# A linear-attention and gated-FFN kernel: the first segment with tokens on partitions, and every engine's list made anew

## The chip, the cores and the metric

The kernel runs on one core of a Trainium2 chip, as one program. The metric is the device time of an execution in microseconds. The engines are TensorE (PE, with its weight loads PEld), VectorE (DVE), ScalarE (ACT), GpSimd (POOL) and SyncE (SP), which issues all DMAs here.

## The reference

Four batches, eight heads, 768 tokens, head size 48. A complex decay is clamped in magnitude, a state of 48x48 per head runs over the tokens, and its output goes through a gated FFN (d_model 384, d_ff 1024) with a three-tap convolution over the tokens.

```python
mag = np.sqrt(a_re * a_re + a_im * a_im)
scale = np.minimum(mag, 0.999) / (mag + 1e-06)
a_re_n, a_im_n = (a_re * scale, a_im * scale)
for t in range(S):
    new_re = ar * S_re - ai * S_im
    new_im = ar * S_im + ai * S_re
    kv = np.einsum('bhd,bhe->bhde', k[:, :, t], v[:, :, t])
    S_re, S_im = (new_re + kv, new_im)
    y[:, :, t] = np.einsum('bhd,bhde->bhe', q[:, :, t], S_re)
...
h = np.maximum(x @ w_in, 0.0)
for k in range(K):
    conv_out += conv_w[k][None, None, :] * hp[:, k:k + S, :]
gate = 1.0 / (1.0 + np.exp(-conv_out))
return (h * gate @ w_out).astype(np.float32)
```

## The kernel before

The recurrence is computed in chunks of 128 tokens. The decays become running sums: of the logarithm of the magnitude, and of the angle. A k or q is multiplied by the exponential of the log sum and by cosine and sine of the angle sum; then a chunk is ordinary causal attention (scores, mask, values) and a state that is carried from chunk to chunk.

Two chunks, 256 tokens, make a segment; there are twelve, three per batch. A segment goes through `a_pre` (load a, squares), `a_log` (logarithms, their running sum, table of logarithms and exponentials), `a_trig` (arctangent), `c_pre` (running sum of the angle, reduced to turns), `c_exp` (exponentials of plus and minus the log sum, times q and k) and `c_post` (cosine, sine, the products `qkc_t`). In nearly all segments channels lie on the partitions (16 channels of each of 8 heads, three groups `g`), and a running sum is a scan along the free dimension on DVE. The first two segments, those in `CUM`, have tokens on the partitions when a is loaded and make their sums as matmuls with a triangle of ones (`sums`, L460), which puts channels on the partitions in the result.

The attention needs q and k with head channels on the partitions (`stk`, 96 rows by head by token). `c_post` gets there through DRAM: it writes `qkc_t` to `qkd` (L596) and reads it back rearranged into `stk` (L598), once for k and once for q. `c_chunk` also transposes k on PE (L612) to `kn`, tokens on partitions, for the state matmuls (L619). `attention` (L656) does scores (L652), mask (L667), values and state (L676), and writes the FFN's input as a high and a low half: `x[0]` by a copy on ACT (L702), `x[1]` by a subtraction on DVE (L703).

The FFN works in ten units of 256 or 384 tokens (`UNITS`); each has four steps, a front (`moe_front`: x times w_in L758, Relu, convolution) and a back (`moe_back`: tanh, gate, times w_out L793). Unit 0 can begin when the token behind its last one is there, that is after chunk 2, the first of segment 1. The weights are loaded and split into high and low halves in the first 75 us (`load_weights`): of 16 splits the first 8 (`WHI`, all of w_in) make their high half on DVE (L387), the others on ACT (L389).

The order of the instructions on each engine is written out by hand: `ORDER` lists them by number for PE, DVE, ACT, POOL and SP, and `in_order` chains them. The first two segments are done eagerly (`FASTP`), and segments run ahead of the units that need them. The ACT's tables are loaded where a listed function needs another one.

Buffers that count here: one for a (`AB`), one for qk (`QB`), two for `qkc_t` (`QC`), three for `stk` (`TB`), two banks for `ps` (`PSA`), which transposes, scores and outputs share.

Of the kernel before, what the change touches and what calls it, by code (L numbers as in the profile page):

```python
# [14 lines left out]
I32 = mybir.dt.int32  # L15
# [63 lines left out]
CUM = [0, 1]  # L79
GROUPS = [1]*len(SEGS)  # L80
# [22 lines left out]
WHI = 8  # L103
# [59 lines left out]
    "DVE": [105, 24, 106, 111, 57, 112, 107, 63, 58, 59, 28, 113, 69, 29, 70, 109, 71, 60, 64, 65, 117, 46, 66, 72,  # L163
# [92 lines left out]
def in_order(tc):  # L256
# [4 lines left out]
    for eng, line in ORDER.items():  # L261
        last, run, sets = None, None, {}
        for k in line:
            if found[k][1]:
                both = [t for t in run[1] if t in found[k][1]] if run else []
                run = (run[0], both) if both else (k, list(found[k][1]))
                sets[run[0]] = run[1][0]
# [809 lines left out]
```

## Time and profile before

| | |
|---|---|
| median of 3 runs | 385.73 us (384.69 to 386.15) |
| profiled execution | 385.09 us |
| its span, first to last instruction | 383.3 us |
| mean granted TensorE clock | 0.971 |
| moved by DMA | 81.12 MB |
| ACT table loads | 42 (41 of them placed by `in_order`, L272) |

Busy time says what share of the span an engine had an instruction in it; matmuls are pipelined, and a busy PE is not a PE at its peak. A row of the timeline gives start, duration, engine, line and tiles, and in brackets how long the engine had been idle and what ended that. "Landing" is the time from the issue of a DMA to its completion.

### The profile page before, as it was taken

Reading aid. Unit: us, or ns where it says so; the run is one execution under the profiler, and the core shown is the slowest. Engines: PE = TensorE matmul, PEld = TensorE weight load, DVE = VectorE, ACT = ScalarE, POOL = GpSimd, SP = SyncE. Lnnn points to the kernel's source line nnn. Section 1 sums busy time; section 2 is a strip of 40 time slices with the busy share of each in tenths; the row PEclk is TensorE's granted clock in tenths of the full one; section 3 lists DMA queues with packets and bytes.
Section 4 is the critical chain, followed back from the end, with each engine's and each line's share of the span. In section 5 each row is a group of like instructions: output and inputs, shape, how many; then the busy total and the mean of one; then the engine's idle time right before and its main releaser. Section 6 shows DMA issues by size and latency. Waiting matters only on the chain.

```text
span 383.3 us, 12048 instructions
## 1 busy us (share of the span) xinstructions
PE 345.3 (90%) x5220; PEld 323.5 (84%) x5220; DVE 337.3 (88%) x552; ACT 333.1 (87%) x566; POOL 6.9 (2%) x42
## 2 busy tenths in 40 slices
PE   2577277899999999999999999999999999999993
PEld 1566275789999999999998998999999899999993
DVE  3999999989999989999999989898999988567680
ACT  5999999989999999999999998999999965346561
POOL 5000000000000000000000000000000000000000
PEclk9989758999999999999999999999999999999999
DMA  7999989995894957975959566974849828101011
GB/s 285 346 365 345 246 290 254 313 225 198 316 265 165 271 132 292 280 210 235 250 170 289 120 234 264 218 236 167 213 146 301 284 109 213 53 3 65 1 44 50
DMA packets 33423, 81.12 MB, mean 212 GB/s; under 512 B 2128, under 2 KB 23632, under 8 KB 31824
## 3 DMA queue, kind: packets, MB, share of 16 engines
q1 hardware_dynamic: 33360, 80.25, 68.4%
q8 instruction: 43, 0.70, 0.8%
q14 instruction: 20, 0.16, 0.1%
HBM read 56.65 MB, written 23.59 MB: 209 GB/s over the span
## 4 chain that ended last, share of the span: by engine, by line
PE 83%; ACT 7%; DVE 6%; issue 1%; DMA 1%; DVEq 0%
PE h_ps L758 27%; PE o L793 27%; PE ps L676 10%; PE ps L652 9%; PE s_ps L619 4%; PE ps L612 3%; PE o L471 2%; ACT w_t L420 2%; ACT L272 1%; ACT x_t L420 1%; DMA a_t<-in_at 1%; DVE qkc_t L592 1%; ACT w_t L484 1%; DVE p_t L667 1%; DVE x_t L497 0%
## 5 line engine op out<-in xcount | busy, mean ns | idle before, releaser
L793 PE MATMUL o<-wo,hg 128*128 128x384 f32 x576 | 122.3, 342 | 0.5 <-issue 0.4
L758 PE MATMUL h_ps<-x,wi 128*128 128x258 f32 (+1 forms) x720 | 122.4, 308 | 0.0
L758 PEld LDWEIGHTS h_ps<-x,wi 128*128 128x128 f32 x720 | 109.2, 189 | 1.1 <-ACT h_t L762 0.3
L793 PEld LDWEIGHTS o<-wo,hg 128*128 128x128 f32 x576 | 98.6, 188 | 3.1 <-issue 1.1
L272 ACT ACT_TABLE_LOAD x41 | 52.6, 1283 | 0.7
L652 PE MATMUL ps<-stk 96*64 96x128 f32 (+1 forms) x768 | 39.8, 257 | 9.9 <-DMA stk<-qkd 8.2
L652 PEld LDWEIGHTS ps<-stk 96*64 96x64 f32 x768 | 36.0, 142 | 14.8 <-ACT kn L613 10.8
L420 ACT ACTIVATE g_t<-g_t,cw 128x256 f32<-128x256 f32 (+1 forms) x80 | 42.5, 550 | 5.1 <-DVE g_t L765 4.9
L763 DVE SCALAR_TENSOR_TENSOR g_t<-h_t,cw 128x256 f32<-128x256 f32 (+1 forms) x80 | 41.6, 532 | 5.1 <-ACT h_t L762 4.9
L762 ACT ACTIVATE h_t<-h_ps 128x258 f32<-128x258 f32 (+1 forms) x80 | 33.5, 426 | 13.4 <-PE h_ps L758 13.1
L765 DVE SCALAR_TENSOR_TENSOR g_t<-h_t,cw,g_t 128x256 f32<-128x256 f32 (+1 forms) x80 | 41.8, 533 | 1.1
L592 DVE TENSOR_TENSOR qkc_t<-w_t,zz_t 128x1536 f32<-128x1536 f32 x24 | 41.7, 1751 | 0.3
L777 DVE SCALAR_TENSOR_TENSOR g_t<-g_t,h_t 128x512 f32<-128x512 f32 (+1 forms) x40 | 31.6, 791 | 5.7 <-ACT g_t L420 5.6
L786 DVE TENSOR_TENSOR hg<-g_t,hg 128x512 fp32r<-128x512 f32 (+1 forms) x40 | 31.6, 791 | 2.5 <-ACT hg L783 2.4
L783 ACT ACTIVATE hg<-g_t 128x512 fp32r<-128x512 f32 (+1 forms) x40 | 28.5, 716 | 5.9 <-DVE g_t L777 5.5
L667 DVE TENSOR_TENSOR p_t<-ps,mask 128x384 f32<-128x384 f32 x48 | 26.1, 552 | 7.4 <-PE ps L652 6.3
L676 PE MATMUL ps<-p_t,v_t 128*32 128x64 f32 x1344 | 25.7, 223 | 2.6 <-issue 1.7
L676 PEld LDWEIGHTS ps<-p_t,v_t 128*32 128x32 f32 x1344 | 23.0, 112 | 3.7 <-issue 2.2
L676 PE MATMUL ps<-stk,s_sb 96*32 96x128 f32 x640 | 22.1, 275 | 0.6 <-issue 0.4
L612 PE MATMUL ps<-ident,qkc_t 128*128 128x128 f32 x120 | 20.2, 289 | 1.4 <-DMA stk<-qkd 1.1
L484 ACT ACTIVATE w_t<-a_t 128x1536 f32<-128x1536 f32 x12 | 17.9, 1489 | 3.9 <-DMA a_t<-in_at 3.9
L577 DVE TENSOR_TENSOR w_t<-w_t,qk_t 128x1536 f32<-128x1536 f32 x12 | 21.0, 1752 | 0.0
(100 smaller groups left out, 450.8 us busy)
## 6 DMA issues: line engine op xcount, KB each, us to landing
qkd<-qkc_t SPq DMA_DIRECT2D x24, 768.0 KB, 4.2
stk<-qkd SPq DMA_DIRECT2D x24, 768.0 KB, 7.6
v_t<-in_v SPq DMA_DIRECT2D x12, 1024.0 KB, 8.7
qk_t<-in_qk SPq DMA_DIRECT2D x12, 768.0 KB, 6.0
a_t<-in_a SPq DMA_DIRECT2D x10, 768.0 KB, 5.1
out<-os_t SPq DMA_DIRECT2D x24, 192.0 KB, 4.5
hg<-in_w_out SPq DMA_DIRECT2D x8, 384.0 KB, 5.4
h_t<-in_w_in SPq DMA_DIRECT2D x8, 384.0 KB, 4.9
```

What stands on the lines that cost most here:

```text
L272: row = [nc.scalar.preload_act_table_set(sets[k]).ins] + row
L420: nc.scalar.activation(out, in_, func=func, **kw)
L592: nc.vector.tensor_tensor(out=qkc, in0=e[:, q:q + 1].broadcast_to([128, 2, NG * w]), in1=zz, op=ALU.mult)
L612: nc.tensor.transpose(tr[:, g - lo], kv[:, g // NG, g % NG], ident)
L652: nc.tensor.matmul(o, lhsT=kt[:, 2 * i + u, part * HC + r:part * HC + r + TM], rhs=qt[:, 2 * i + u, part * HC:C], start=first, stop=part = ...
L676: nc.tensor.matmul(yp[r0:r0 + 32, q // 4, cols], lhsT=left, rhs=right, start=r0 not in started, stop=stop, tile_position=(0, r0), skip_gro ...
L758: nc.tensor.matmul(hp, lhsT=wi[iw][:, f, kt], rhs=x[ix][:, kt], start=(k == 0), stop=(k == 8))
L762: nc.scalar.activation(h, hp, func=AF.Relu)
L763: nc.vector.scalar_tensor_tensor(out=g, in0=h[:, 0:n], scalar=cw[:, f, 0:1], in1=h[:, 1:n + 1], op0=ALU.mult, op1=ALU.add)
L765: nc.vector.scalar_tensor_tensor(out=g, in0=h[:, 2:n + 2], scalar=cw[:, f, 2:3], in1=g, op0=ALU.mult, op1=ALU.add)
L777: nc.vector.scalar_tensor_tensor(out=g, in0=g, scalar=1.0, in1=h[:, :, 1:n + 1], op0=ALU.add, op1=ALU.mult)
L793: nc.tensor.matmul(ops[t][:min(C, n - t * C)], lhsT=hg[:, k, t * C:min((t + 1) * C, n)], rhs=w[:, fw], start=(f == 0 and i == 0), stop=(f ...
```

## The change

Segment 0 alone (`TOK = [0]`) keeps tokens on the partitions up to the end. Its a and its q and k (`qk0`) come laid out by token from the host. Its running sums have the triangle as the stationary operand (`token_sums`, two output tiles, one per chunk), and the totals that later chunks need come from small matmuls (`totals`). The carry at the start of a batch, a constant, is now the bias of the exponentials instead of a matmul; segment 1 keeps its carry matmuls. q and k by heads come from PE transposes, four heads at a time, evacuated by ACT (k) and DVE (q); there is no write to DRAM and no read back for this segment, and the untransposed k serves the state matmuls as it is. The two chunks of the segment are produced and attended to one after the other. The a tile of segment 0 is loaded and squared in two halves. The first table load is put in front of ACT's first instruction. All high halves of weights are made on ACT (`WHI = 0`). Units, segments and buffers are as before; `ORDER` is a new list for every engine.

```diff
+TOK = [0]
-WHI = 8
+WHI = 0
...
+        if sets:
+            sets[line[0]] = sets.pop(next(iter(sets)))
...
+    base = {1: filled("base", SIGN * L0), -1: filled("nbase", -SIGN * L0)}
...
+    def token_sums(x, tiles):
+        xv = x.rearrange("t (k c) -> t k c", k=2)
+        for k in range(2):
+            for i in range(k + 1):
+                nc.tensor.matmul(tiles[k], lhsT=tri[0][:, (k - i) * C:(k - i + 1) * C], rhs=xv[:, i], start=i == 0,
+                                 stop=i == k)
+        return tiles
+    def totals(x, ps):
+        xv = x.rearrange("t (k n g) -> t k n g", k=2, g=NG)
+        ends = ps.shape[2]
+        for g in range(NG):
+            for k in range(2):
+                c0 = k if ends == 2 else 0
+                nc.tensor.matmul(ps[:, g, c0:], lhsT=xv[:, k, :, g], rhs=tri[0][:, C - 1::C][:, c0 + 2 - ends:],
+                                 start=k == 0, stop=k == 1, skip_group_check=True)
...
-            nc.sync.dma_start(at_, at0[CUM.index(p)])
+            for i in range(2) if p == 0 else (slice(0, 2),):
+                nc.sync.dma_start(at_[:, i], at0[CUM.index(p)][:, i])
...
-        nc.scalar.activation(w, at_, func=AF.Square)
+        for i in range(2) if p == 0 else (slice(0, 2),):
+            nc.scalar.activation(w[:, i], at_[:, i], func=AF.Square)
...
+        if p in TOK:
+            nc.vector.tensor_tensor(out=w[:, 1], in0=w[:, 1], in1=w[:, 0], op=ALU.subtract)
+            st["l", p] = token_sums(w[:, 1], [psO.tile([128, 512], F32, name=f"o{k}")[:, 0:CH] for k in range(2)])
...
+            totals(w[:, 1], ends)
+            nc.scalar.activation(cl[:, b, :, j + 1:j + 1 + m], ends, func=AF.Identity, bias=base[1])
...
+            tiles = token_sums(x[:, 0], [psH.tile([128, 512], F32, name="h_ps")[:, 0:CH] for k in range(2)])
...
+    def c_token(p, k, e, zz):
+        b, j, m = segs[p]
+        if k == 0:
+            st["stk"] = [at.tile([128, H, PR], F32, name="stk", bufs=TB)[0:96] for q in range(2)]
+        stk, found = st["stk"], {}
+        for q in (1, 0):
+            x = sc.tile([128, 2, NG * PR], F32, name="qkc_t", bufs=QC).rearrange("p c t -> p (c t)")[:, 0:2 * CH]
...
+            for i in range(2):
...
+                tr = psA.tile([128, 4, 128], F32, name="ps")
+                for h in range(4):
+                    nc.tensor.transpose(tr[0:96, h], found[q][:, 4 * i + h], ident)
+                d = stk[q][:, 4 * i:4 * i + 4, k * C:(k + 1) * C]
+                if q:
+                    nc.scalar.copy(out=d, in_=tr[0:96])
+                else:
+                    nc.vector.tensor_copy(d, tr[0:96])
...
+        c_chunk(b * NC + j + k, None, [s[:, :, k * C:(k + 1) * C] for s in stk], st["v"], found[1])
```

In the new SP list both halves of a come first, then the weights; the load of `qk0` stands behind the first five loads of w_in and four of w_out, and the load of v for segment 0 behind the last of w_in. In the new ACT list the Arctan of segment 0 comes before the last logarithm and the log sums.

## Rows read from the trace of the kernel before

**Rows 1.** The page, busy us (share of the span) and instructions.
```profile
PE 345.3 (90%) x5220; PEld 323.5 (84%) x5220; DVE 337.3 (88%) x552; ACT 333.1 (87%) x566; POOL 6.9 (2%) x42
```

**Rows 2.** Stretches: length, busy us by engine, PE clock, DMA share, GB/s.
```profile
33.00:50.00 17.00, 6.21 (x85) 5.24 (x85) 16.39 (x29) 16.79 (x25) 0.00 (x0) 0.81 0.96 268
50.00:67.00 17.00, 13.87 (x310) 11.40 (x306) 16.53 (x29) 16.11 (x24) 0.00 (x0) 0.70 1.06 286
75.00:300.00 225.00, 222.64 (x3512) 210.85 (x3513) 213.70 (x319) 220.69 (x370) 1.23 (x12) 1.00 0.76 228
```

**Rows 3.** The chain of waits: start us, us, what.
```profile
0.80 4.57 DMA a_t<-in_at
5.38 1.48 ACT w_t L484
...
115.02 0.81 PE ps L612 x6
...
368.49 8.47 PE o L793 x48
```

**Rows 4.** Timeline, ACT and PE, up to the first front.
```profile
0.80 1.28 ACT L484 ACT_TABLE_LOAD   x1 [0.80 <-PEq L1067]
...
6.88 1.28 ACT L272 ACT_TABLE_LOAD   x1
...
13.53 2.90 PE L471 MATMUL o<-tri,w_t 128*128 128x256 f32 x8 [8.08 <-DVE w_t L502]
...
16.49 1.48 ACT L484 ACTIVATE w_t<-a_t 128x1536 f32<-128x1536 f32 x1 [0.59 <-DMA a_t<-in_at]
...
19.68 1.49 ACT L420 ACTIVATE w_t<-w_t 128x1536 f32<-128x1536 f32 x1 [0.40 <-DVE gm L485]
...
20.94 2.13 PE L471 MATMUL o<-tri,x_t 128*128 128x256 f32 x12
...
32.25 0.17 ACT L395 ACTIVATE cl<-o 128x2 f32<-128x2 f32 x1 [0.30 <-PE o L471]
...
61.87 0.49 ACT L702 ACTIVATE x<-ps 128x384 fp32r<-128x384 f32 x1 [0.76 <-PE ps L676]
...
72.33 0.49 ACT L702 ACTIVATE x<-ps 128x384 fp32r<-128x384 f32 x1
...
74.91 2.40 PE L758 MATMUL h_ps<-x,wi 128*128 128x258 f32 x18
```

**Rows 5.** Timeline of SP, and the stk tile from 45 to 75 us.
```profile
50.99 0.32 SPq L596 DMA_DIRECT2D qkd<-qkc_t  x1
...
53.40 5.49 SPq L598 DMA_DIRECT2D stk<-qkd  x2
...
DMA to landing us min/median/max: 8.3/9.1/10.8
```

**Rows 6.** Groups by line and shape: busy us, mean ns.
```profile
L592 DVE TENSOR_TENSOR qkc_t<-w_t,zz_t 128x1536 f32<-128x1536 f32 x24 | 41.7, 1751 | 0.3
...
L613 ACT COPY kn<-ps 128x512 f32<-128x512 f32 x20 | 12.1, 603 | 0.1
...
L613 ACT COPY kn<-ps 128x256 f32<-128x256 f32 x20 | 8.0, 400 | 0.0
...
L389 ACT ACTIVATE wo<-hg 128x384 fp32r<-128x384 f32 x8 | 4.1, 517 | 0.0
...
L387 DVE TENSOR_SCALAR wi<-g_t 128x384 fp32r<-128x384 f32 x8 | 2.8, 356 | 0.0
```

**Rows 7.** The page, DMA issues of the whole run: KB, median us to landing.
```profile
qkd<-qkc_t SPq DMA_DIRECT2D x24, 768.0 KB, 4.2
stk<-qkd SPq DMA_DIRECT2D x24, 768.0 KB, 7.6
```

More of the change, by code (lines that the diff above doesn't have):

```diff
@@ L108 @@
 ORDER = {
[54 rows of a table removed]
-    "DVE": [105, 24, 106, 111, 57, 112, 107, 63, 58, 59, 28, 113, 69, 29, 70, 109, 71, 60, 64, 65, 117, 46, 66, 72,
[26 rows of a table removed]
-    "ACT": [23, 26, 27, 25, 30, 108, 152, 114, 199, 202, 38, 41, 37, 43, 203, 40, 206, 42, 156, 154, 201, 159, 161,
[26 rows of a table removed]
-    "POOL": [186, 2, 187, 13, 3, 19, 21, 15, 4, 17, 0, 7, 1, 8, 16, 20, 18, 6, 5, 14, 9, 11, 10, 12, 405, 404, 616,
[8 rows of a table removed]
[54 rows of a table added]
+    "DVE": [28, 105, 106, 111, 112, 57, 58, 59, 32, 63, 113, 64, 69, 107, 70, 33, 71, 61, 46, 65, 47, 35, 115, 67,
[27 rows of a table added]
+    "ACT": [27, 26, 29, 30, 31, 152, 60, 114, 34, 108, 72, 66, 156, 154, 208, 38, 210, 41, 40, 43, 211, 42, 212, 215,
[26 rows of a table added]
+    "POOL": [183, 2, 184, 13, 3, 21, 23, 15, 4, 19, 0, 7, 1, 8, 16, 22, 20, 6, 5, 14, 9, 11, 10, 12, 17, 18, 414,
[8 rows of a table added]
 }
@@ L280, in linear_attention_moe_kernel @@
 @with_exitstack
-def linear_attention_moe_kernel(ctx: ExitStack, tc: tile.TileContext, a, at0, qk, v, w_in, conv_w, w_out, out):
+def linear_attention_moe_kernel(ctx: ExitStack, tc: tile.TileContext, a, at0, qk, qk0, v, w_in, conv_w, w_out, out):
     nc = tc.nc
@@ L503, in a_log @@
             tact(w[:, 0], x[:, 1], func=AF.Ln, scale=1e-6, bias=one1)
+        if p in TOK:
+            nc.vector.tensor_tensor(out=w[:, 1], in0=w[:, 1], in1=w[:, 0], op=ALU.subtract)
+            st["l", p] = token_sums(w[:, 1], [psO.tile([128, 512], F32, name=f"o{k}")[:, 0:CH] for k in range(2)])
+            st["t", p] = psO.tile([128, 512], F32, name="o2")
+            ends = st["t", p][:, 0:2 * NG].rearrange("p (g k) -> p g k", k=2)
+            totals(w[:, 1], ends)
+            nc.scalar.activation(cl[:, b, :, j + 1:j + 1 + m], ends, func=AF.Identity, bias=base[1])
+            st["x", p], st["w", p] = x, w
+            return
         if p in CUM:
-            st["l", p] = sums(("o0", "o1"), cl[:, b, :, j], ((w[:, 1], 0), (w[:, 0], 1)))
+            st["l", p] = sums(("o0", "o1"), cl[:, b, :, j] if j else None, ((w[:, 1], 0), (w[:, 0], 1)))
             for lo, hi, ps in st["l", p]:
-                small_copy(SM, cl[:, b, lo:hi, j + 1:j + 1 + m], ps[:, :, C - 1::C])
+                nc.scalar.activation(cl[:, b, lo:hi, j + 1:j + 1 + m], ps[:, :, C - 1::C], func=AF.Identity,
+                                     **({} if j else {"bias": base[1]}))
             st["x", p], st["w", p] = x, w
@@ L524, in load_qk @@
             st["qk", p] = seg_tile(ld, p, "qk_t", QB)
-            load_seg(st["qk", p], qk, p)
+            if p in TOK:
+                nc.sync.dma_start(st["qk", p], qk0[TOK.index(p)])
+            else:
+                load_seg(st["qk", p], qk, p)
     def c_pre(p):
@@ L536, in c_pre @@
         turns = zz[:, 0].bitcast(I32)
-        if p in CUM:
+        if p in TOK:
+            tiles = token_sums(x[:, 0], [psH.tile([128, 512], F32, name="h_ps")[:, 0:CH] for k in range(2)])
+            for k, ps in enumerate(tiles):
+                tv, zv = (t[:, k * CH:(k + 1) * CH] for t in (turns, zz[:, 1]))
+                nc.scalar.activation(tv, ps, func=AF.Copy, scale=INV_2PI)
+                nc.vector.scalar_tensor_tensor(out=zv, in0=ps, scalar=INV_2PI, in1=tv, op0=ALU.mult,
+                                               op1=ALU.subtract)
+            end = st["t", p][:, 8:8 + NG]
+            totals(x[:, 0], end.unsqueeze(2))
+            whole = sc.tile([128, NG], I32, name="whole", bufs=1)
+            part = sc.tile([128, NG], F32, name="part", bufs=1)
+            nc.scalar.activation(whole, end, func=AF.Copy, scale=INV_2PI)
+            nc.vector.scalar_tensor_tensor(out=part, in0=end, scalar=INV_2PI, in1=whole, op0=ALU.mult,
+                                           op1=ALU.subtract)
+        elif p in CUM:
             for lo, hi, ps in sums(("o2", "o1"), cth, ((x[:, 0], 0),)):
@@ L556, in c_pre @@
             nth = sc.tile([128, NG], F32, name="cth", bufs=3)
-            small_copy(SM, nth, z[:, :, m * C - 1], TWO_PI)
+            small_copy(SM, nth, part if p in TOK else z[:, :, m * C - 1], TWO_PI)
             st["cth", p] = nth
@@ L568, in c_exp @@
         load_qk(p)
-        x, qkt = st["x", p], st.pop(("qk", p))
+        x, qkt, j = st["x", p], st.pop(("qk", p)), segs[p][1]
         e = st["e", p] = st.pop(("w", p))
@@ L574, in c_exp @@
                 continue
+            if p in TOK:
+                for k, ps in enumerate(st["l", p]):
+                    tact(e[:, i, k * CH:(k + 1) * CH], ps, func=AF.Exp, scale=sign,
+                         **({} if j else {"bias": base[round(sign * SIGN)]}))
+                continue
             for lo, hi, ps in st["l", p]:
-                tact(e[:, i].rearrange("p (g t) -> p g t", g=NG)[:, lo:hi], ps, func=AF.Exp, scale=sign)
+                tact(e[:, i].rearrange("p (g t) -> p g t", g=NG)[:, lo:hi], ps, func=AF.Exp, scale=sign,
+                     **({} if j else {"bias": base[round(sign * SIGN)]}))
         nc.vector.tensor_tensor(out=e, in0=e, in1=qkt, op=ALU.mult)
@@ L588, in c_post @@
         w = C * m
+        if p in TOK:
+            return e, zz
         stk, kv = [None, None], None
@@ L602, in c_post, with c_chunk @@
                     [s[:, :, k * C:(k + 1) * C] for s in stk], st["v"])
-    def c_chunk(c, kv, stk, vt):
+    def c_token(p, k, e, zz):
[5 more added lines that the diff above has]
+            x = sc.tile([128, 2, NG * PR], F32, name="qkc_t", bufs=QC).rearrange("p c t -> p (c t)")[:, 0:2 * CH]
+            nc.vector.tensor_tensor(
+                out=x.rearrange("p (n c g) -> p c n g", c=2, g=NG), op=ALU.mult,
+                in0=e[:, q:q + 1, k * CH:(k + 1) * CH].broadcast_to([128, 2, CH]).rearrange("p c (n g) -> p c n g", g=NG),
+                in1=zz[:, :, k * CH:(k + 1) * CH].rearrange("p c (n g) -> p c n g", g=NG))
+            found[q] = x.rearrange("p (h r) -> p h r", h=H)
+            for i in range(2):
+                seg_time(p, OP + .8 + 4 * k + 1.6 * (1 - q) + .8 * i)
+                tr = psA.tile([128, 4, 128], F32, name="ps")
[4 more added lines that the diff above has]
+                    nc.scalar.copy(out=d, in_=tr[0:96])
+                else:
+                    nc.vector.tensor_copy(d, tr[0:96])
+        seg_time(p, OP + 3.5 + 4 * k)
+        c_chunk(b * NC + j + k, None, [s[:, :, k * C:(k + 1) * C] for s in stk], st["v"], found[1])
+    def c_chunk(c, kv, stk, vt, kn=None):
         b, j = divmod(c, NC)
-        if j < NC - 1:
+        if j < NC - 1 and kn is not None:
+            state(c, kn, vt)
+        elif j < NC - 1:
             kn = sc.tile([128, H, 96], F32, name="kn", bufs=KB)
@@ L613, in c_chunk, with state @@
                 nc.scalar.copy(out=knv[:, :, lo:hi], in_=tr[:, :hi - lo].rearrange("s c x -> s x c"))
+            state(c, kn, vt)
+        st["att", c] = (stk, vt)
+    def state(c, kn, vt):
+        b, j = divmod(c, NC)
+        if True:
             if j == 0:
@@ L628, in c_chunk @@
             st["s", c] = ss
-        st["att", c] = (stk, vt)
     def blocks(i):
@@ L836, in eager, with attend @@
         return n < FASTP
-    def attend(p):
+    def attend(p, only=None):
         nonlocal loaded_u
         b, j, m = segs[p]
-        for c in range(b * NC + j, b * NC + j + m):
+        for c in range(b * NC + j, b * NC + j + m) if only is None else (b * NC + j + only,):
             attention(c)
@@ L848, in finish @@
         for p in grp(n):
-            c_post(p)
-            attend(p)
+            found = c_post(p)
+            for k in range(segs[p][2]) if found else ():
+                c_token(p, k, *found)
+                attend(p, k)
+            if not found:
+                attend(p)
     def start(n):
@@ L1041, in prepare @@
     first = [divmod(p, NP) for p in CUM]
-    at0 = np.stack([np.stack([grp(ar), grp(ai)])[:, b, :, j].transpose(3, 0, 2, 4, 1, 5) for b, j in first])
+    at0 = np.stack([np.stack([grp(ar), grp(ai)])[:, b, :, j].transpose(*((3, 0, 2, 1, 5, 4) if p in TOK else
+                                                                       (3, 0, 2, 4, 1, 5))).reshape(C, 2, NG * PR)
+                    for p, (b, j) in zip(CUM, first)])
+    qk0 = np.stack([np.stack([grp(inputs["q"]), grp(inputs["k"])])[:, b, :, j].transpose(3, 0, 2, 1, 5, 4)
+                    for b, j in (divmod(p, NP) for p in TOK)])
     qk = np.ascontiguousarray(np.stack([grp(inputs["q"]), grp(inputs["k"])]).transpose(1, 3, 2, 7, 0, 6, 4, 5))
@@ L1054, in prepare @@
         "qk": qk.reshape(B, NP, 128, 2, NG * PR),
+        "qk0": np.ascontiguousarray(qk0).reshape(len(TOK), C, 2, NG * PR),
         "v": v.reshape(B, NP, C, 2, 4 * VW),
```

229 rows, old and new, of the table ORDER are left out of this document.

## The prediction

> **What bounds the kernel now.** I read the page's busy shares first, then the stretches, then the chain of waits, then the timeline of the first 80 us. All three compute engines are busy for 87 to 90% of the span [rows 1], which says nothing yet; the stretches do. Between 33 and 67 us TensorE (PE) is busy for 6.2 and 13.9 of 17 us at a granted clock of 0.81 and 0.70, while VectorE (DVE) and ScalarE (ACT) have 16.1 to 16.8 us of work in each 17. From 75 to 300 us PE is busy for 222.6 of 225 us at a clock of 1.00 [rows 2]. The chain of waits ends in a block of PE matmuls (368.49 to 376.96 us) [rows 3]. So there are two regimes: a start of 75 us set by the lists of ACT and DVE, and a run of PE that begins with the first front matmul (74.91 us) [rows 4] and ends at 376.96, 302.0 us later. Behind it 6.3 us remain to the end of the span (383.3) and 1.8 us lie around the span (profiled execution 385.09).
>
> A microsecond gained in the start counts only if that first front matmul comes earlier or PE has less left to do behind it. PE's new list has the same instructions in front of that matmul as the old one, apart from the first segment's own: sums, transposes and scores of segments 0 and 1, scores of chunk 3. What is left behind it is the same. The run itself can give back at most PE's idle time in it, 2.4 us in rows 2.
>
> What sets 74.91? Unit 0 needs token 256, so chunk 2, so segment 1, which still takes the way through DRAM. In the timeline the second qkc tile of segment 1 is written out at 50.99, the two stk reads are issued between 53.40 and 58.9, and they take 8.3 to 10.8 us, so the later one is there at about 67.7 [rows 5]: 16.7 us for the round trip, with the DMA engines booked at 106% [rows 2]. Then come scores, masks and values, ACT copies chunk 2 to x at 72.33 [rows 4], and PE reaches the front 2.6 us later. DVE and ACT are without a gap all that time; data, DVE and ACT arrive within a few us of each other.
>
> **The change part by part: DMA.** It removes four transfers of 768 KB (two qkd, two stk) of segment 0, 3.1 MB. Between 33 and 67 us the chip moves 268 to 286 GB/s [rows 2], so 11 us of booked DMA time go. The round trip of segment 1 then goes nearer to the medians of the whole run, 4.2 plus 7.6 us [rows 7], with the two reads side by side say 12.5 us. The q tile must be ready first: in the new DVE list it stands behind the four small qkc tiles of segment 0, two of its four head copies, two masks and an x of chunk 0; I come to 51.9 us by adding the list up. Landing 64.4 instead of 67.7: 3.3 us earlier on this one path.
>
> **ACT up to the x copy of chunk 2.** This is the sum I go by, because ACT's list is followed to the letter and is full. What stands in front of that copy is the old list plus the following. Neighbouring instructions overlap by about 0.09 us, so an instruction counts its duration less that. Eight high-half copies of w_in come over from DVE, at 0.517 us each [rows 6]: 8 x 0.43 = +3.5. Four evacuations of transposed heads (96x512) replace two of 512 and two of 256 columns (0.603, 0.400) [rows 6]: +0.4. The Square in two halves: +0.1. Exponentials, turns and the small copies have the same columns in another cut: 0. The first table load of 1.28 us, at 6.88 between Square and Ln [rows 4], moves to the front, where ACT waits for the DMA anyway, and the load at 0.80 that was there falls away: -1.3. Work: +2.7 us.
>
> Against that stands idle time. Square starts at 5.38, when 768 KB have landed [rows 3]. Half of it should be there about 1.2 us sooner (half of the 4.57 us of that load [rows 3] would be 2.3 less, nothing 0; I take the middle); the second half, issued behind the first, is there about 0.5 us after the first Square, as I estimate: -0.7. Four waits of ACT inside the stretch, 0.59, 0.40, 0.30 and 0.76 us, together 2.05 [rows 4], belong to the old order. Adding the new lists up side by side I find two places where ACT stands: before the exponentials, and 0.3 us before the Ln of segment 3. The first depends on PE. Sums over tokens are three matmuls of 384 columns behind six small ones. Twelve records, six matmuls of mean 192 columns, took 2.13 us, and eight records took 2.90 in the slower case [rows 4]: 0.71 to 1.45 us per matmul of 384, so 2.1 to 4.4 us for three. ACT then waits 0.3 to 2.6; nearer to the lower, since the angle sums have run shortly before: 0.5. So 0.8 replaces 2.05: -1.25. Sum: 2.7 - 0.7 - 1.25 = +0.75 us; x at 73.1, front at 75.7. Bounds: all old waits stay, half a tile lands no sooner, and PE is slow: +2.7 + 0.5 + 2.6 = +5.8; no waits at all and the full 2.3 us: +2.7 - 2.3 - 2.05 = -1.7.
>
> **DVE.** Eight copies at 0.356 [rows 6] leave: -2.2 net of overlap. One subtraction of two 768-column tiles comes (half of a qkc tile's 1.751 [rows 6]): +0.9; four head copies as ACT's of 512 columns, 0.603 [rows 6], say 0.65: +2.2; four qkc of half size for two: +0.1. Together +1.0, but the first instruction, the sum of squares, may start with the weights instead of behind them; by my sum of its list the last mask of chunk 2 is done at 70.4. DVE stays just in front of ACT.
>
> **PE.** Carry matmuls of segment 0 go, 32 head transposes come for 12 (0.135 us each, from six in 0.81 us [rows 3]): +2.7; the sums come out about even, fewer wide ones against twelve small ones. All of it lies between 12 and 60 us, where PE was idle for 10.8 us of the one 17 us stretch [rows 2]: nothing. If that cover were gone it would be +2.7.
>
> **SP.** v of segment 0 moves behind the last w_in loads, to about 24 us; it is needed for the state at about 33, a 1 MB load. If it takes over 9 us, state, q transposes and head copies of chunk 0 shift by the excess; DVE and ACT have about 1 us of cover there. The qk load moves behind weights and is used at 28. Segment 2's qk load waits for segment 1's product (42), as before.
>
> **The moved high halves.** The rows say ACT takes 0.517 where DVE took 0.356. The Trainium skill, page "ScalarE: Activation LUTs", section "Rules for kernel authors", goes against the move: simple arithmetic belongs on VectorE, not ScalarE. By that rule the eight copies make the late engine later, and nothing else is recovered; the trace agrees in the duration.
>
> **Rivals.** *Slower: ACT is late.* If the waits of the old list come back in new places and the token sums run at half clock, the first front is up to 5.8 us late; it decides as soon as ACT's x copy passes 74.2 (72.33 and half a per cent). Price halfway from the sum to that bound: +3.3, 388.4 us. For it: ACT is busy for 16.8 and 16.1 of 17 us [rows 2] and receives the most work, and the log sums of segment 0 now come only after its Arctan with two switches of tables. Against: by the lists the exponentials of segment 0 are done 5 us before DVE comes to their product. 22%.
>
> *Faster: the DMA path was the limit.* If ACT and DVE have enough slack in the new list to follow the earlier landing, the front moves by 3.3 us: 385.1 - 3.3 = 381.8 us. For it: the landing at 67.7 really precedes the scores, and segment 0's own round trip, of the same kind, is gone altogether. Against: between the kn copies and x the new list has two Sines, an Arctan, an Exp with its table load and a Square of later segments, all to be done first. 33%.
>
> *Same* is what the sum says: 3 us of DMA gain are covered by ACT, which has just as much more to do. 45%.
>
> **Numbers.** 385.09 + 0.75 = 385.8 against the profiled execution, which lies 0.6 below the median of three (385.73); against the median it would be 386.5. I take 386.0. Half a per cent, 1.9 us, is about what a measurement of this kernel can tell from no change. The range reaches to most of the fast and of the slow case: 381.0 to 389.0; the likeliest alone is 384.2 to 387.8. Faster 0.33, same 0.45, slower 0.22.
>
> **What would show it.** Right: the first front matmul at 75 to 77 us; ACT over 95% busy from 6 to 75 us; stk of segment 1 landed by 65 and lying there until 67 or later; DMA below 100% from 40 to 60; about 302 us from first front to the last matmul; 41 table loads. Wrong, to the fast side: a first front before 73, or a PE run under 300 us. Wrong, to the slow side: ACT idle for over 3 us between 12 and 60 us, or a state of chunk 0 that waits for v.

## The result, and the profile after

| | before | after |
|---|---|---|
| median | 385.94 us (384.69 to 386.38, 4 runs) | 390.98 us (389.60 to 392.05, 4 runs) |
| ratio to before, 95% interval | | 1.0143 (1.0106 to 1.0180) |
| profiled execution, its span | 385.09, 383.3 us | 389.60, 387.9 us |
| first front matmul, end of the last matmul | 74.91, 376.96 us | 79.57, 381.18 us |
| ScalarE's copy of chunk 2 to x | 72.33 us | 77.63 us |
| moved by DMA | 81.12 MB | 77.98 MB |

The change makes the kernel 5.0 us slower, beyond the predicted range and on the side that had 22%. TensorE's run from the first front to the last matmul is 301.6 us long (before 302.05), so the loss lies in the first 80 us.

ScalarE's timeline of the kernel after, the rows in which it had stood idle (in brackets: how long, and what ended it), and the copy of chunk 2; they answer to [rows 4]:

```profile
3.96 0.84 ACT L510 ACTIVATE w_t<-a_t 128x768 f32<-128x768 f32 x1 [1.88 <-DMA a_t<-in_at]
...
11.38 0.84 ACT L425 ACTIVATE x_t<-x_t 128x768 f32<-128x768 f32 x1 [0.24 <-DVE x_t L523]
...
19.14 0.27 ACT L536 ACTIVATE cl<-o,base 128x6 f32<-128x6 f32 x1 [0.48 <-PE o L497]
...
22.71 1.05 ACT L425 ACTIVATE w_t<-o,nbase 128x384 f32<-128x384 f32 x2 [2.39 <-issue]
...
36.32 0.18 ACT L542 ACTIVATE cl<-o 128x4 f32<-128x4 f32 x1 [2.16 <-PE o L476]
...
41.69 1.48 ACT L510 ACTIVATE w_t<-a_t 128x1536 f32<-128x1536 f32 x1 [0.35 <-DVE qkc_t L673]
...
57.41 1.48 ACT L510 ACTIVATE w_t<-a_t 128x1536 f32<-128x1536 f32 x1 [0.66 <-DVE qkc_t L653]
...
77.63 0.48 ACT L796 ACTIVATE x<-ps 128x384 fp32r<-128x384 f32 x1
```

The waits behind the first Square's add up to 0.24 + 0.48 + 2.39 + 2.16 + 0.35 + 0.66 = 6.28 us, where the old order had 2.05. The one marked "issue" shows no releaser, but it ends as TensorE ends segment 0's log sums (18.90 + 3.72 = 22.62), which those exponentials read. TensorE's timeline of the same stretch, and the first front:

```profile
12.37 3.57 PE L486 MATMUL h_ps<-x_t,tri 128*128 128x384 f32 x6 [12.37 <-ACT x_t L425]
16.74 2.30 PE L497 MATMUL o<-tri,w_t 128*128 128x2 f32 x12 [0.80 <-DVE w_t L531]
18.90 3.72 PE L486 MATMUL o<-w_t,tri 128*128 128x384 f32 x6
26.13 2.08 PE L476 MATMUL o<-cl,ident 128*128 128x256 f32 x4 [3.51 <-ACT w_t L425]
28.00 2.56 PE L497 MATMUL o<-tri,x_t 128*128 128x1 f32 x12
30.42 2.91 PE L476 MATMUL o<-tri,w_t 128*128 128x256 f32 x8
33.12 1.06 PE L476 MATMUL o<-cl,ident 128*128 128x256 f32 x2
33.97 3.62 PE L476 MATMUL o<-tri,w_t 128*128 128x256 f32 x16
37.43 1.04 PE L682 MATMUL ps<-ident,qkc_t 128*96 128x128 f32 x8
...
79.57 0.62 PE L852 MATMUL h_ps<-x,wi 128*128 128x258 f32 x3
```

Read it as one line in which each piece stands behind the piece above it: log totals, log sums, segment 1's first carry matmuls (after 3.51 us without work, because they need the bank that the last exponential frees, and that one is listed behind a 1.49 us logarithm), angle totals, segment 1's sums, and only then chunk 0's transposes. VectorE's timeline shows who pays as well:

```profile
27.48 0.56 DVE L528 TENSOR_SCALAR w_t<-w_t 128x768 f32<-128x768 f32 x1 [2.44 <-ACT x_t L425]
...
39.34 1.00 DVE L673 TENSOR_TENSOR qkc_t<-w_t,zz_t 128x768 f32<-128x768 f32 x1 [3.04 <-PE s_ps L714]
```

The first is ScalarE's wait handed on; the second is the place of chunk 0's transposes, and of the state matmuls that follow them, behind segment 1's sums. From 39 us on VectorE has no gap up to the first front. Stretches of the kernel after (busy us of PE, PEld, DVE, ACT, POOL, then granted clock, DMA share, GB/s), against [rows 2]:

```profile
16.00:33.00 17.00, 12.76 (x42) 10.15 (x43) 14.50 (x36) 14.07 (x22) 0.00 (x0) 0.68 0.85 298
33.00:50.00 17.00, 14.47 (x242) 12.47 (x241) 13.96 (x24) 14.44 (x26) 0.00 (x0) 0.92 0.45 169
50.00:67.00 17.00, 9.61 (x136) 7.71 (x136) 17.00 (x28) 16.30 (x24) 0.00 (x0) 0.60 0.85 274
```

DMA is relieved as predicted, 0.45 and 0.85 for 0.96 and 1.06, while ScalarE and VectorE, which [rows 2] shows full from 33 to 50 us, now stand idle for 2.5 to 3.0 us in each of the first two stretches. SyncE's timeline and the page show the round trip of segment 1, as in [rows 5] and [rows 7]:

```profile
55.73 2.00 SPq L657 DMA_DIRECT2D qkd<-qkc_t  x2
59.34 4.04 SPq L659 DMA_DIRECT2D stk<-qkd  x2
```

```profile
qkd<-qkc_t SPq DMA_DIRECT2D x22, 768.0 KB, 4.1
stk<-qkd SPq DMA_DIRECT2D x22, 768.0 KB, 6.9
```

The second product is ready at 57.4 us (before 51.0), the last read is issued at 63.1 and lands 6.7 us later, at 69.8: 12.4 us instead of 16.7, but begun 6.4 us later.

### The profile page after: what moved, and what is told of

The parts are those of the page before. It is cut to its first block, busy times and chain, and to the rows that moved or that the text cites. A ratio compares the mean times of both kernels' runs of the same rounds, so it can differ in the third digit from the quotient of the medians.

```text
span 387.9 us, 12100 instructions
## 1 busy us (share of the span) xinstructions
PE 349.3 (90%) x5234; PEld 326.4 (84%) x5234; DVE 338.7 (87%) x552; ACT 335.7 (87%) x574; POOL 7.9 (2%) x44
## 2 busy tenths in 40 slices
DMA packets 31713, 77.98 MB, mean 201 GB/s; under 512 B 2081, under 2 KB 22049, under 8 KB 30113
## 4 chain that ended last, share of the span: by engine, by line
PE 83%; DVE 6%; ACT 5%; issue 2%; DMA 1%; SPq 0%
PE h_ps L852 27%; PE o L887 27%; PE ps L770 10%; PE ps L746 9%; PE s_ps L714 4%; PE ps L701 3%; PE o L476 2%; ACT w_t L425 2%; DMA hg<-in_w_out 1%; PE o L497 1%; DVE qkc_t L653 1%; ACT L276 1%; DVE g_t L354 1%; DVE g_t L356 0%; DVE x_t L523 0%
## 5 line engine op out<-in xcount | busy, mean ns | idle before, releaser
L653 DVE TENSOR_TENSOR qkc_t<-w_t,zz_t 128x1536 f32<-128x1536 f32 x22 | 38.2, 1753 | 2.5 <-ACT zz_t L425 2.4
L770 PE MATMUL ps<-stk,s_sb 96*32 96x128 f32 x640 | 23.4, 290 | 0.2
L510 ACT ACTIVATE w_t<-a_t 128x1536 f32<-128x1536 f32 (+1 forms) x13 | 18.0, 1384 | 3.1 <-DMA a_t<-in_at 2.0
L701 PE MATMUL ps<-ident,qkc_t 128*128 128x128 f32 x108 | 18.3, 282 | 2.4 <-issue 1.4
```

The source lines that it names most:

```text
L653: nc.vector.tensor_tensor(out=qkc, in0=e[:, q:q + 1].broadcast_to([128, 2, NG * w]), in1=zz, op=ALU.mult)
L770: nc.tensor.matmul(yp[r0:r0 + 32, q // 4, cols], lhsT=left, rhs=right, start=r0 not in started, stop=stop, tile_position=(0, r0), skip_gro ...
```

## The experiments

Theory 1: the loss is the waiting of ScalarE and VectorE for TensorE's line between 16 and 38 us. Rival 2: ScalarE's eight extra high-half copies. Rival 3: VectorE, without a gap from 39 us, sets the end. All times are medians; the ratios are to the kernel before, run beside each kernel. Its medians there were 385.94 us (after), 385.39 (E1 to E4), 385.84 (E5 to E8) and 385.61 (E9 to E12), so small differences between groups go by the ratios. The first front is that of the profiled execution. In the lists 153 is segment 0's angle sums, 36 its log sums, 37 its log totals, 158 its angle totals; 216, 220 segment 1's first carry matmuls, 217 to 221 the rest of its sums; on ScalarE 38 copies the log totals, 40 to 43 are segment 0's exponentials, 211 segment 1's logarithm. A matmul leaves two records in these traces (E4's 17 added ones leave 34): the twelve records of a set of totals are six matmuls, the six of segment 0's log sums are three.

| run | us | ratio (95%) | first front, us |
|---|---|---|---|
| after | 390.98 | 1.0143 (1.0106 to 1.0180) | 79.57 |
| E1 high halves back on VectorE | 393.92 | 1.0225 (1.0182 to 1.0268) | 84.19 |
| E2 sums ahead of totals | 389.54 | 1.0122 (1.0083 to 1.0161) | 78.55 |
| E3 angle totals later | 394.18 | 1.0222 (1.0183 to 1.0261) | 82.67 |
| E4 17 idle-time matmuls | 394.17 | 1.0209 (1.0168 to 1.0251) | 77.60 |
| E5 new order | 386.70 | 1.0026 (1.0005 to 1.0047) | 75.91 |
| E6 E5 with 16 such matmuls | 390.03 | 1.0082 (1.0053 to 1.0110) | 76.13 |
| E7 E5, high halves on GpSimd | 392.11 | 1.0160 (1.0138 to 1.0182) | 80.08 |
| E8 before, high halves on ScalarE | 386.51 | 1.0017 (0.9994 to 1.0041) | 76.53 |
| E9 first half of E5 | 388.35 | 1.0068 (1.0037 to 1.0099) | 77.42 |
| E10 second half of E5 | 387.18 | 1.0050 (1.0022 to 1.0078) | 75.10 |
| E11 E5, later lines changed too | 390.94 | 1.0169 (1.0130 to 1.0207) | 75.27 |
| E12 E11 with 9 such matmuls | 392.61 | 1.0215 (1.0172 to 1.0258) | 76.58 |

**E1.**

```diff
-WHI = 0
+WHI = 8
 "DVE": ... 59,
+       60,
```

(and so for 66, 72, 78, 84, 90, 96, 102, each taken from ScalarE's list.)

> The changed kernel with one part undone: the eight high halves of w_in stand on VectorE again, each behind the conversion that it reads. Theory 1 (the loss is ScalarE's and VectorE's waiting for TensorE's sums between 16 and 38 us): five of the eight copies stand ahead of 30 us and so in front of those waits, which then only grow; the three later ones give ScalarE 1.5 us and cost VectorE 1.0 us; 390 to 391.5 us, as the changed kernel (391.0). Rival 2 (ScalarE's eight extra copies are the loss): 8 x 0.43 = 3.5 us come back, 387.5 us. Rival 3 (VectorE, without a gap from 39 us on, sets the end): only slower, up to 8 x 0.35 = 2.8 us, 394 us.

2.9 us slower than the kernel after. Rival 2's 387.5 does not come: ScalarE without the copies waits longer (2.52 and 3.23 us for the same two sums, and 1.29 us for the angle sums), and everything of VectorE's is later. As this run also loads VectorE, it is E5, which leaves the copies on ScalarE, that drops rival 2. Theory 1 had said "no change" and missed: VectorE is as full as rival 3 says. That VectorE's work is not the loss itself, E5 shows, which leaves it as it is.

**E2.**

```diff
-"PE": [153, 37, 36, 216, ...
+"PE": [153, 36, 37, 216, ...
-"ACT": ... 208, 38, 210, 41, 40, 43, 211, 42, ...
+"ACT": ... 208, 210, 41, 40, 43, 38, 211, 42, ...
```

> The changed kernel with segment 0's three log sums ahead of its twelve log totals on TensorE, and the totals' copy on ScalarE behind the four exponentials. Theory 1: the sums that the exponentials wait for end 2.2 us earlier (at 20.5 instead of 22.6 us), ScalarE's waits of 0.48 and 2.39 us shrink to about 0.7, and everything behind them moves by 2: 389 us. Rivals 2 and 3 (ScalarE's copies, VectorE's work): no change, 391 us.

1.4 us faster than after by the medians, but the two intervals overlap, so the time alone does not show a gain; the first front came 1.0 us earlier, and the waits of 0.48 and 2.39 became one of 1.23. The sums end at 19.04, but the first two exponentials overwrite the half of `w_t` that the totals read, and so begin at 21.05, when the totals are through. That told what E5 needs.

**E3.**

```diff
-"PE": ... 216, 220, 158, 217, ... 172, 174, 231, ...
+"PE": ... 216, 220, 217, ... 172, 174, 158, 231, ...
-"ACT": ... 159, ... 170, ...
+"ACT": ... 170, 159, ...
```

(161 on ScalarE and 160 on VectorE, which read them, move behind 177 and 175.)

> The changed kernel with segment 0's twelve angle totals on TensorE behind segment 1's sums and chunk 0's turns instead of ahead of them; their readers on ScalarE and VectorE move behind too. Theory 1: segment 1's log sums begin at 28.2 instead of 30.4 us, ScalarE's wait of 2.16 us for them goes and VectorE's wait of 3.04 us shrinks to about 1: 389 us. Rivals 2 and 3: no change, 391 us.

3.2 us slower: the wait for segment 1's sums went, but segment 1's angle sums carry on from these totals. ScalarE waited 2.72 us for the totals and 1.80 us for those angle sums, VectorE 2.05 and 1.43. The place was right to suspect and the direction wrong: the totals have to go earlier.

**E4.**

```diff
+WARM1 = {153: 8, 37: 3}
+WARM2 = {216: 6}
...
+            DUM.append(nc.tensor.matmul(ps[:, 128:384], lhsT=ident, rhs=tri[0], start=True, stop=True,
+                                        skip_group_check=True).ins)
```

(that many matmuls, read by nothing, ahead of those groups on TensorE.)

> The changed kernel with 17 matmuls of 128x256 that nothing reads added on TensorE: 8 ahead of segment 0's angle sums, 3 ahead of its log totals, 6 ahead of segment 1's first sums, where the engine stood idle. Theory 1 in the form that the half clock of those sums makes the waits: the granted clock of 16 to 33 us goes from 0.68 to over 0.9, the log sums take 1.9 instead of 3.7 us, ScalarE's waits of 2.39 and 2.16 and VectorE's of 2.44 and 3.04 us shrink to under 1 each: 387 us (386 to 388.5). If the order of the sums in TensorE's line is the cause and not the clock: 390 us. Rivals 2 and 3: 391 us.

The first front came 2.0 us earlier, and the time is 3.2 us longer, which none of the forecasts had. Stretches of this kernel:

```profile
16.00:18.00 2.00, 1.22 (x7) 1.22 (x8) 2.00 (x4) 2.00 (x5) 0.00 (x0) 1.00 1.02 387
18.00:20.00 2.00, 2.00 (x8) 1.70 (x9) 2.00 (x5) 1.44 (x3) 0.00 (x0) 0.57 1.04 333
20.00:24.00 4.00, 4.00 (x9) 2.31 (x8) 4.00 (x15) 1.14 (x4) 0.00 (x0) 0.50 0.72 259
24.00:28.00 4.00, 4.00 (x18) 3.21 (x16) 1.08 (x4) 4.00 (x5) 0.00 (x0) 0.86 0.85 270
28.00:32.00 4.00, 4.00 (x24) 3.79 (x24) 3.93 (x8) 3.94 (x7) 0.00 (x0) 1.00 0.69 237
```

The matmuls put in from 6 to 16 us did not hold the clock: it fell to 0.50 (the lower of the two levels, 1.2 GHz) behind the log totals, twelve records of one or two columns, and the log sums took 4.19 us. It was back by 28 us, where segment 1's last sixteen records took 2.78 instead of 3.62 us, and ScalarE's wait of 2.16 us went, VectorE's of 3.04 fell to 0.25. So faster sums of segment 1 are worth 2 us of the loss in the start; the slow log sums this run left as they were. Of what the run behind the first front lost (307.5 us instead of 301.6), 3.1 us are stops of TensorE, told at the end; for the rest I have no cause.

**E5.**

```diff
-"PE": [153, 37, 36, 216, 220, 158, 217, ...
+"PE": [153, 36, 37, 158, 216, 220, 217, ...
-"ACT": ... 208, 38, 210, 41, 40, 43, 211, 42, ...
+"ACT": ... 208, 210, 40, 41, 38, 42, 43, 211, ...
-for i, sign in ((1, -SIGN), (0, SIGN)):
+for i, sign in ((0, SIGN), (1, -SIGN)) if p in TOK else ((1, -SIGN), (0, SIGN)):
```

> The changed kernel with one new order around segment 0's sums: on TensorE the three log sums, the twelve log totals, then at once the twelve angle totals, and only then segment 1's first carry matmul; on ScalarE the two exponentials that overwrite nothing which the totals read come first, then the totals' copy, then the other two, and the logarithm of segment 1 behind all four. Theory 1 (ScalarE's and VectorE's waits for TensorE's line between 16 and 38 us are the loss): ScalarE's waits of 0.48, 2.39 and 2.16 us and VectorE's of 2.44 and 3.04 us shrink to 0.5 or less each, the first front matmul comes at 75.5 instead of 79.6 us, 387 us. If what is gained there is lost again in later waits, 390 us. Rivals 2 and 3 (ScalarE's copies, VectorE's work): 391 us.

386.70 us: 4.3 of the 5.0 us are back, with the same instructions on the compute engines. Timeline of ScalarE and TensorE in this kernel (its line numbers are lower by one):

```profile
21.11 0.27 ACT L535 ACTIVATE cl<-o,base 128x6 f32<-128x6 f32 x1 [0.22 <-PE o L496]
...
52.40 1.49 ACT L509 ACTIVATE w_t<-a_t 128x1536 f32<-128x1536 f32 x1 [0.67 <-DVE qkc_t L652]
...
73.32 0.49 ACT L795 ACTIVATE x<-ps 128x384 fp32r<-128x384 f32 x1 [0.60 <-PE ps L769]
```

```profile
16.95 2.20 PE L485 MATMUL o<-w_t,tri 128*128 128x384 f32 x6 [0.35 <-DVE w_t L530]
...
21.43 2.34 PE L496 MATMUL o<-tri,x_t 128*128 128x1 f32 x12 [0.36 <-ACT cl L535]
...
25.85 2.92 PE L475 MATMUL o<-tri,w_t 128*128 128x256 f32 x8 [0.16 <-DVE w_t L527]
...
75.91 2.70 PE L851 MATMUL h_ps<-x,wi 128*128 128x258 f32 x20
```

Segment 1's sums begin 4.6 us earlier, the exponentials follow ScalarE's other work without a gap, VectorE's 2.44 and 3.04 us are 0 and 0.17. Theory 1 holds, and by its size the loss is this. The order also sets how fast the log sums run: ahead of the totals they took 2.20 us, behind them 3.72. So E5 does not part the standing in line from the slow sums; both came with the order.

**E9 and E10** are E5 in halves: E9 has only 158 moved ahead of 216 (37 stays ahead of 36), E10 all of E5 but that.

```diff
 E9
-"PE": [153, 37, 36, 216, 220, 158, 217, ...
+"PE": [153, 37, 36, 158, 216, 220, 217, ...
 E10
-"PE": [153, 37, 36, 216, 220, 158, 217, ...
+"PE": [153, 36, 37, 216, 220, 158, 217, ...
```

> The changed kernel with one half of the new order alone: segment 0's angle totals go into TensorE's idle time of 22.6 to 26.1 us, ahead of segment 1's first carry matmul instead of behind it. Theory 1: segment 1's sums begin at 28.2 instead of 30.4 us, ScalarE's wait of 2.16 us for them goes, VectorE's 3.04 us shrink to about 1, and its waits of 0.48 and 2.39 us stay: 2 us faster, 389 us. If the two halves of the new order only work together: 391 us.

> The changed kernel with the other half of the new order alone: segment 0's log sums ahead of its log totals, the two exponentials that overwrite nothing the totals read first, the logarithm of segment 1 behind all four; the angle totals stay where the change put them. Theory 1: ScalarE's waits of 0.48 and 2.39 us shrink to 0.5 together, segment 1's sums begin some 1.5 us earlier: 2 to 2.5 us faster, 388.7 us. If the two halves only work together: 391 us.

2.6 and 3.8 us faster than after, and 4.3 together: each works alone, and they overlap by 2. The intervals of E10 and E5 overlap, so it is not shown that E9's half adds anything to E10's. In E9 the first two waits stay (0.73 and 2.86 us) and the later ones, for segment 1's sums and chunk 0's turns, are 0 and 0.25.

**E6** is E5 with such matmuls as in E4.

```diff
+WARM1 = {153: 8, 36: 3}
+WARM3 = {216: 3, 217: 2}
```

> The order of the run before with 16 matmuls of 128x256 that nothing reads: 8 ahead of segment 0's angle sums, 3 ahead of its log sums, 3 ahead of segment 1's first carry matmul, 2 ahead of the rest of its sums. If the half clock still costs something behind the new order: segment 1's sums take 4 instead of 6.5 us, VectorE's wait for chunk 0's turns goes and the time falls by 1, to 386 us; if the order alone was the loss, 387 us as without them; if TensorE's gaps at 140 and 300 us grow as in the run with 17 such matmuls, 390 us, and the first front matmul shows the start's share alone.

The first front is where E5 has it (76.13, 75.91), with the clock of 16 to 33 us at 0.90 instead of 0.80: once the order is right the lower clock there costs the start nothing. The time is 3.3 us longer by the medians and 2.2 by the ratios, nearly all of it behind the first front.

**E7** is E5 with the eight copies on GpSimd.

```diff
+            elif split[0] < 8:
+                nc.gpsimd.tensor_scalar(hi, wb.bitcast(F32), 1.0, None, op0=ALU.mult)
```

(the eight leave ScalarE's list for GpSimd's.)

> The new order of the run before last with the eight high halves of w_in on GpSimd, which stands idle from 6 to 80 us. If ScalarE's list is what sets the start once the waits are gone (its eight copies were 3.5 us): 2 to 3 us faster than the new order alone, 384.5 us, faster than the kernel before. If VectorE's list sets it as much: 386.5 us. If GpSimd's copies hold up VectorE's subtractions behind them or slow VectorE: 390 us or more.

5.4 us slower than E5. The groups by line of GpSimd, 6 to 80 us:

```profile
L393 POOL TENSOR_SCALAR wi<-g_t 128x384 fp32r<-128x384 f32 x8 | 13.4, 1685 | 40.1 <-DVE g_t L355 40.1
```

A copy takes 1.69 us there, for 0.52 and 0.36 in [rows 6], and VectorE waits 1.07 and 2.19 us for it ahead of two subtractions.

**E8** is the kernel before with the eight copies on ScalarE.

```diff
-WHI = 8
+WHI = 0
```

(each group moves from VectorE's list to the place in ScalarE's that it had in time.)

> The kernel before with that one part of the change: the eight high halves of w_in go from VectorE to ScalarE, each into ScalarE's line at the time that it had on VectorE. By the prediction's term (8 x 0.43 us on an engine over 95% busy): 3.5 us slower, 389.4 us. By the run with the copies put back, where VectorE was the fuller engine: no slower than 386, as ScalarE's 3.5 us more stand against VectorE's 2.8 us less.

0.7 us slower; the interval holds no change at all and ends at 0.4%, 1.6 us. So the change's part that the prediction costed highest, +3.5 us on ScalarE, costs less than half of that as a part, with 2.8 us less for VectorE to do [rows 6]. (The profiled execution, 387.68 us, was the slowest of this kernel, so its first front is a late one.)

**E11** is E5 with the end of the start listed anew; **E12** is E11 with nine matmuls that nothing reads.

```diff
-"ACT": ... 253, 255, 394, 393, 273, 259, 368, 391, 257, 261, 447, 138, 582, 586, 270, 583, 274, 275, ...
+"ACT": ... 253, 255, 259, 261, 394, 393, 273, 368, 391, 257, 447, 138, 270, 582, 274, 275, 586, 583, ...
-"DVE": ... 395, 265, 398, 267, 448, 143, 271, ...
+"DVE": ... 265, 395, 267, 398, 271, 448, 143, ...
 E12
+WARM = {199: 5, 201: 2, 258: 2}
```

> The new order (both halves) with the lines of 62 to 74 us changed as well: ScalarE copies chunk 2's four key banks in a row ahead of segment 2's sine and cosine, and chunk 2's output ahead of the next segment's exponential and square; VectorE applies chunk 2's two masks ahead of the two products of segment 2. It asks whether the start's end still follows the waits once the first ones are gone: TensorE's wait of 2.24 us for those copies goes and the first front matmul comes 2 us earlier, 384.7 us, faster than the kernel before. If TensorE at the lower clock sets that stretch, or the two products are then late: 386.7 us, as the new order alone.

> The kernel of the run ahead of this with 9 matmuls of 128x256 that nothing reads, 5, 2 and 2 of them in TensorE's idle times of 50 to 53, 55 and 62 us. In the new order TensorE's granted clock is 0.57 in 67 to 75 us. If that half clock costs there what it costs in its matmuls (scores 2.64 instead of 1.56 us, values 3.66 instead of 2.05): 2 us faster than without them, 383 us. If the copies and masks of ScalarE and VectorE set that stretch: no change against the run ahead.

The first front comes 0.6 us earlier in E11 and the time is 4.2 us longer, against both forecasts. Three rows of E11's timeline:

```profile
65.38 0.88 ACT L701 COPY kn<-ps 128x512 f32<-128x512 f32 x2 [1.41 <-PE s_ps L713]
...
72.46 0.50 ACT L795 ACTIVATE x<-ps 128x384 fp32r<-128x384 f32 x1 [1.40 <-PE ps L769]
...
80.22 0.84 PE L851 MATMUL h_ps<-x,wi 128*128 128x258 f32 x3 [2.66 <-ACT h_t L855]
```

I had taken a wait away from TensorE and given two of 1.4 us to ScalarE, whose sines are then 2.6 us late, and 5 us behind the first front TensorE waits 2.66 us for ScalarE's Relu; for the rest of the 4.2 us I have no cause. An early first front is worth nothing when ScalarE's list is late. E12 raised the clock of 50 to 67 us from 0.61 to 0.86 and gained nothing (the intervals overlap): the lower clock does not set that stretch. None of the versions beats the kernel before; of those with the change E5 is nearest.

## Why the prediction was wrong, point by point

**The two regimes** were right: the run behind the first front kept its length (301.6 us, "about 302").

**The sum for ScalarE's copy of chunk 2** is where it failed. It said +0.75 us; it was +5.30:

| term | forecast | measured |
|---|---|---|
| first Square, in halves | -0.7 | -1.42 + 0.17 = -1.25 |
| work | +2.7 | +2.3 |
| waits in place of 2.05 | 0.8 - 2.05 = -1.25 | 6.28 - 2.05 = +4.23 |

(Work is what remains of 5.30.) Start and work together came out 0.95 us better than forecast; the waits 5.5 us worse. The failed step is the one that reads "I find two places where ACT stands": there were six. Of the one before the exponentials it took 0.5 where its own bound, 2.6, was nearly right (2.39); the other that it named, 0.3 us before the Ln of segment 3, came as 0.66 us before that segment's Square. The log sums ran in the slow case of [rows 4] (3.72 us), behind the totals and at a granted clock of 0.65 from 18 to 20 us and 0.50 from 20 to 22. What the sum did not contain at all is that TensorE is a list too. I had worked out how long each sum takes and not what stands in front of it in TensorE's line, nor which exponential frees the bank that the next sum needs. E5 shows that the other terms together were nearly right: with most of the waits gone the copy comes at 73.32 us (forecast 73.1), the first front at 75.91 (75.7), and the time is 386.7 (386.0).

**"PE: nothing"**, since TensorE was idle for 10.8 us of one stretch, is the same error from the other side: idle time elsewhere is no cover for work that others wait for. The chain of waits of the kernel after runs from 16 to 38 us mostly on TensorE (the "issue" piece is the wait that its log sums end):

```profile
16.74 2.30 PE o L497 x12
20.32 2.39 issue
22.71 3.38 ACT w_t L425 x5
26.13 2.08 PE o L476 x4
28.21 2.35 PE o L497 x12
30.56 7.04 PE o L476 x26
```

**VectorE**: the work came out as said, +1.1 us up to chunk 2's subtraction for +1.0, but 5.48 us of waits (2.44 and 3.04) came for 0.73.

**DMA**: right in mechanism and size, 12.4 us for the round trip (forecast 12.5), and useless, since the q tile was ready at 57.4 instead of 51.9 us.

**v** held nobody up: no wait of the state of chunk 0 shows it. 41 table loads, as said. "ACT over 95% busy from 6 to 75 us" was 90%, and the sign for the slow side, over 3 us of idle ScalarE between 12 and 60, is there with 6.0 us.

**The rivals.** The slower one named the mechanism, old waits in new places with token sums at half the clock; its price of 388.4 was too low and its bound of +5.8 holds the copy's +5.30. The faster one fell with the late q tile, and E5 answers it: there the last read of segment 1 is issued at 58.07 us and lands 6.4 us later, at 64.5 (forecast 64.4), and the first front still comes at 75.91. So the earlier landing alone moves nothing.

**The rule weighed against the trace.** The Trainium skill, page "ScalarE: Activation LUTs", section "Rules for kernel authors", puts simple arithmetic on VectorE and not on ScalarE. The durations agree with it (0.36 us on VectorE, 0.52 on ScalarE [rows 6]), the times do not follow it for the eight copies: on VectorE they made the changed kernel 2.9 us slower (E1), on ScalarE the kernel before at most 0.4% slower (E8). I take it that what counts is whose list is the later one, not whose instruction is shorter; no run tests that reason by itself.

## What to carry to other kernels

When two engines are full and a third is half idle, walk through the third one's line in order before calling its work free: a wait of the full ones for it can be a loss that no later slack returns. Small matmuls that produce a carry belong in the gap before the next consumer's sums, not between those sums and what they need; and of several instructions that wait for the same result, list first the one that overwrites nothing still being read. Judge a new order by the lists of all full engines some way past the milestone, not by the milestone: E11's came earlier and its kernel later.

## What the runs showed of the hardware

TensorE stops in the middle of a stream of matmuls without a wait that the profile shows ("issue"), at a place fixed by the count of its instructions. Timeline of the kernel after, and of E4:

```profile
297.68 0.97 PE L770 MATMUL ps<-p_t,v_t 128*32 128x64 f32 x56
298.57 0.55 PE L701 MATMUL ps<-ident,qkc_t 128*128 128x128 f32 x3
300.56 0.33 PE L701 MATMUL ps<-ident,qkc_t 128*128 128x128 f32 x1 [1.44 <-issue]
```

```profile
298.29 0.56 PE L782 MATMUL ps<-p_t,v_t 128*32 128x64 f32 x25
301.36 0.93 PE L782 MATMUL ps<-p_t,v_t 128*32 128x64 f32 x31 [2.51 <-issue]
```

After 56 + 3 = 59 records in the one and 25 in the other: 34 earlier, and E4's 17 added matmuls are 34 records. E6 (32 records added) stops after 27, E12 (18) after 41. (E7, with none added, stops after 55; why, I cannot say.)

The DMA queues show what ends these stops. One queue (q8) carries packets of instructions, 16 KB each. The kernel after, first the page, for the whole run, then the DMA view of 298 to 300.6 us (packets, MB, share):

```profile
q8 instruction: 43, 0.70, 0.8%
```

```profile
q8 instruction: 1, 0.02, 3.0%
```

That one packet runs from 298.01 to 299.24 us, and TensorE goes on at 300.56. In E4 it runs from 298.71 to 299.91, and TensorE goes on at 301.36. It is so in all 14 traces: each of TensorE's 38 stops marked "issue" ends 1.26 to 1.65 us behind the end of such a packet. That leaves little room for anything but a wait for instructions; what makes a packet late no run shows. Most packets hold up nothing: in a run 2 to 5 of the 43 do. The stops over 0.25 us behind the first front add up to 1.9 us in the kernel after, 2.7 in E12, 2.8 in E5, 3.4 in E9, 4.2 in E6 and 4.9 in E4. So added matmuls move the stops, but that they lengthen them is not shown: E9, which has none, has more than E12, which has nine.

The Trainium skill, page "Runtime: NRT & Kernel Launch", section "Instruction fetch mechanics", says that instructions come in blocks while the engine runs and that the cost of a block's boundary is mostly hidden. These traces agree with "mostly"; the stops that are not hidden took up to 2.5 us.

GpSimd's plain copy of 128x384 took 1.69 us, with VectorE busy beside it, more than four times VectorE's 0.36.

In E4 the granted clock fell to its lower level behind twelve records of one or two columns, although wide matmuls had run from 6 to 16 us. But the clock on record does not account for the slow sums by itself. E9's log sums in the timeline, and the stretch that they lie in:

```profile
19.06 4.19 PE L485 MATMUL o<-w_t,tri 128*128 128x384 f32 x6
```

```profile
20.00:24.00 4.00, 4.00 (x12) 2.48 (x10) 4.00 (x13) 1.14 (x4) 0.00 (x0) 1.00 0.70 238
```

They took the same 4.19 us as E4's, behind the same totals, at a granted clock of 1.00 on record (E3's too), against 2.20 us ahead of the totals in E2 and E5. Why they are slow there stays open.
